# Top-32 attention and an MLP mixer on one core: the ninth tile's last columns copied with its group's, and the first pair's last rows in a buffer of their own

## The chip, the cores and the metric

The kernel runs on one core of one Trainium2 chip. The metric is the device time of one execution in microseconds. Times of the engines come from one profiled execution, whose span runs from the first to the last instruction.

## What is computed

Attention in which each query keeps its 32 largest scores, over 8 batches of 8 heads, 576 positions and head size 64; then a mixer over positions and one over channels:

```python
scores = scale * np.matmul(q, k.transpose(0, 1, 3, 2))           # 8 x 8 x 576 x 576
kth = np.partition(scores, -top_k, axis=-1)[..., -top_k:-top_k + 1]   # top_k = 32
scores = np.where(scores >= kth, scores, -1000000000.0)
attn = np.exp(scores - np.max(scores, axis=-1, keepdims=True))
attn = attn / (np.sum(attn, axis=-1, keepdims=True) + 1e-09)
x = np.matmul(attn, v)           # brought to 8 x 576 x 512, the heads side by side
h = np.maximum(x.transpose(0, 2, 1) @ w_tok1, 0.0) @ w_tok2      # 576 -> 256 -> 576
u = x + h.transpose(0, 2, 1)
out = u + np.maximum(u @ w_ch1, 0.0) @ w_ch2                     # 512 -> 1536 -> 512
```

## The kernel before

**Units and tiles.** The work is cut into 32 units (`plan_unit(u)`): a unit is two heads of one batch, so four units are a batch, and unit 31 is the last pair of batch 7. 576 rows are four tiles of 128 (`W` = 512 columns) and a tail of 64 (`TAIL`). The two heads of a unit give eight tiles of 128 query rows; their two tails of 64 rows together make a ninth tile. The score tiles stand in two groups in SBUF: `SS0` with four tiles (g = 0) and `SS1` with five (g = 1, the ninth tile as its last).

**One unit.** `load_one` brings q and k of both heads by three DMAs each: 512 rows of either head and one for the 64 last rows of both. `qk_tr` turns them on TensorE, `qk_tail_tr` the last rows, and `qk_ev`, `qk_tail_ev` copy them out of PSUM into `qkT`. `s1_mm` makes the last 64 columns of a group's four full tiles (eight products in two banks, one for each head), `s0_mm` the first 512 columns of one tile index, `st_mm` the ninth tile: part 0 its 512 columns, part 1 its last 64, each part in a bank of its own. `s1_ev`, `s0_ev` and `st_ev` copy the banks into `SS0` or `SS1`, on ScalarE (ACT) except in the very first group. Then VectorE (DVE) finds the 32nd largest score of each row: `upper`, `split4`, four `top_round`s and a `low_round` for each group, while GpSimd (POOL) makes the lower halves (`both_bits`, `lower_bits`). ACT makes the exponentials (`expo`) and the terms that suppress what lies below the threshold (`below_act`; `steep` with POOL's `sink`); the result is turned by TensorE (`p_tr`, `ptail_tr`, copied out by `p_ev`, `ptail_ev`) or by a DMA (`turn`), `o_mm` multiplies with v, `o_den` and `o_ev` divide. `h1_mm`, `h1_ev`, `ut_mm`, `ut_ev` are the position mixer for the unit's 128 channels.

**After a batch's fourth unit** `plan_mlp` makes the channel mixer: `h2t_mm`, `h2_mm` and their copies, then `out_mm` with `out_ev` (line 796) for five row blocks of 15 products each. For the last batch the order is another: `plan_part_sums` makes the products over the first three units' channels early (`pre_mm`, line 1103, copied by `pre_ev`), and `plan_mlp_last` adds the fourth (`rest_mm`, `join`), makes `h2_last` and accumulates the output (`begin`, `accum`, line 1156). In the last unit's group 1 the selection is applied by `kept` on DVE (line 574).

**PSUM** has eight banks: two `tp`, three `s0`, one `O`, two `mps`. `st_mm` and, except for the very first group, `s1_mm` and `s0_mm` use `s0`; `mps` serves all of the mixers.

**What sets the order.** All work is entered as tasks into a `Plan` with an engine, an estimated duration, a rank and the things that it waits for. `Plan.order` plays this through, taking on each engine the ready task of the lowest rank, and the instructions are emitted in the order that results; on the chip each engine keeps to it, and semaphores make it wait for data and buffers. A rank is 100 x the unit's number plus an entry of `RANK`. For the last batch, the entry `rush` is added for what follows the selection (`V = U + RANK["rush"]`); for batch 6's mixer `rush6` is added. `slack` is time that the plan adds between a task and what waits for it: the entries `q_wait`, `t_wait`, `o_wait` (in tenths of a us) and a constant for the first units. Where the plan sees TensorE idle before a task, it puts in products that nobody reads (`spare`, line 277), in number:

```python
n = int((now - at) * SPARE / SPARE_US)      # SPARE = 0.8, SPARE_US = 0.22
```

While the plan's time is below 80 us (`SETTLED`) these are four products of 128 columns for each n, later one of 512. `at` is 3.0 us at the start (`LEAD`).

`copy` (lines 336 and 338) is the helper that makes the copies on ACT and on DVE, so many steps share these lines. `lists["hx"]` is a buffer in SBUF that `split4` and `top_round` work in.

Of the kernel before, what the change touches and what calls it, by code (L numbers as in the profile page):

```python
# [19 lines left out]
RANK = {  # L20
    "begin_l": -2054, "o_wait": 16, "t_wait": 6, "q_wait": 272, "v_wait": 112, "pre_mm": -34365, "pre_ev": -31279, "rest_mm": 14920,
    "begin": 31546, "flags": 8794, "rush": -6145, "rush6": -3394, "load": -9078, "qk_tr": 7627, "qk_ev": -3163, "st_mm": -8007,
    "st_ev": 896, "keep": 3463, "h1_mm": -30213, "h1_ev": 3666, "ut_mm": -46945, "ut_ev": -3088, "out_mm": 13329, "out_ev": -772,
# [125 lines left out]
def kernel(  # L149
# [138 lines left out]
    def load_one(st, name, src, b, p, queue=None):  # L288
        queue = queue or nc.sync
        t = ldp.tile([P, NS, 2, D], f32, name=name + "L", tag=name + "L")  # L290
        two = slice(2 * p, 2 * p + 2)
        if isinstance(b, int):
            rws = src[b, two, :, :]
        else:
            rws = src[bass.ds(b, 1), two, :, :].rearrange("o h s d -> (o h) s d")
        for hh in range(2):
            queue.dma_start(
                out=t[:, 0:NT, hh, :], in_=rws[hh, 0:W, :].rearrange("(t p) c -> p t c", p=P)
            )
        queue.dma_start(  # L300
            out=t[0:TAIL, NT, :, :], in_=rws[:, W:S, :].rearrange("h p c -> p h c")
        )
        st[name] = t
# [41 lines left out]
    def qk_tail_tr(st, kind="tp"):  # L345
        tails = bank(kind)[:, 0 : 2 * TAIL].rearrange("p (i c) -> p i c", i=2)
        for i, name in enumerate("qk"):
            nc.tensor.transpose(
                tails[:, i, :],
                st[name][0:TAIL, NT, :, :].rearrange("p h d -> p (h d)"),  # L350
# [7 lines left out]
    def s1_mm(st, g, kind="s0"):  # L358
        T = st["T"]
        x = [bank(kind) for hh in range(2)]  # L360
        for a in range(4):
# [7 lines left out]
            )  # L369
        st["s1"] = x  # L370
# [6 lines left out]
    def s1_ev(st, g, hh, eng="ACT"):  # L377
        copy(
            eng,
            s_tile(st, g)[:, hh:4:2, W:S],  # L380
            st["s1"][hh][:, 0 : 2 * TAIL].rearrange("p (a c) -> p a c", a=2),
        )
# [18 lines left out]
    def st_mm(st, part):  # L401
        T = st["T"]
        lo, hi = ((0, W), (W, S))[part]
        x = bank("s0")
        for hh in range(2):
            nc.tensor.matmul(
                out=x[hh * TAIL : (hh + 1) * TAIL, 0 : hi - lo],
                lhsT=T[rows[hh], 0, W:S],
                rhs=T[rows[hh], 1, lo:hi],
                start=True,  # L410
                stop=True,
            )
        st["st", part] = x

    def st_ev(st, part):
        lo, hi = ((0, W), (W, S))[part]
        nc.scalar.copy(out=st["SS", 1][:, 4, lo:hi], in_=st.pop(("st", part))[:, 0 : hi - lo])
# [438 lines left out]
    def plan_unit(u):  # L856
# [6 lines left out]
        for name, src in (("q", q), ("k", k)):  # L863
            aside = u < 2 and name == "k"
            ld[name] = add("ACT" if aside else "SP", 1.75, U - 5000 if aside else U + RANK["load"],
                           lambda name=name, src=src, aside=aside: load_one(st, name, src, b, p, nc.scalar if aside else None),
                           acq=[("ld" + name, u)])
        ev, prev = [], None
        for i in range(2):
            a = add("PE", 0.61, U + RANK["qk_tr"], lambda i=i: qk_tr(st, i), deps=[ld["qk"[i]], prev] + chain.get("first", []), acq=[("tp", u, "q", i)] + ([] if i else [("qkT", u)]), slack=(3.0 if u == 0 else 4.5) if u < 5 else 0.1 * RANK["q_wait"])  # L870
# [18 lines left out]
        for g in range(2):  # L889
            early = u == 0 and g == 0  # L890
            kind = "mps" if early else "s0"
            a = add("PE", 0.65, U + RANK["s_mm" + str(g)] + 10 * g, lambda g=g, kind=kind: s1_mm(st, g, kind), deps=ev + smm[-1:],
# [3 lines left out]
            for hh in range(2):  # L896
                eng = "DVE" if early and hh else "ACT"
                evs.append(
                    add(eng, 0.17, U + RANK["s_ev" + str(g)] + 10 * g, lambda g=g, hh=hh, eng=eng: s1_ev(st, g, hh, eng),
# [15 lines left out]
            if g == 1:  # L915
                for part in range(2):
                    a = add("PE", (1.01, 0.28)[part], U + RANK["st_mm"], lambda part=part: st_mm(st, part),
                            deps=[smm[-1]], acq=[("s0", u, "st", part)],
                            rel=[("qkT", u)] if part else [])
                    smm.append(a)  # L920
                    evs.append(
                        add("ACT", (0.49, 0.12)[part], U + RANK["st_ev"], lambda part=part: st_ev(st, part),
                            deps=[a, e0] + ([evs[-1]] if part else []),
                            rel=[("s0", u, "st", part)])
                    )
# [361 lines left out]
    with tc.If(flag != 0):  # L1287
        with tc.For_i(0, B, 1) as bv:
            mst = {}
            for p in range(NPAIR):  # L1290
# [9 lines left out]
                for g in range(2):  # L1300
# [7 lines left out]
                    if g == 1:  # L1308
                        for part in range(2):
                            st_mm(st, part)  # L1310
                            st_ev(st, part)
# [62 lines left out]
```

## Time and profile before

| | us |
|---|---|
| median of 3 runs (884.36 to 884.5) | 884.5 |
| the profiled execution | 884.62 |
| its span, first to last instruction | 882.8 |
| busy: VectorE (DVE) | 861.7 |
| busy: ScalarE (ACT) | 834.1 |
| busy: TensorE (PE) | 819.8 |
| busy: GpSimd (POOL) | 597.2 |

The profile names the engines PE (TensorE products), PEld (its weight loads), DVE, ACT, POOL and SP (the queue that issues most DMAs); q behind a name is that engine's sequencer. A group line reads: source line, engine, operation, output tile <- input tiles, shapes, count, then busy time in us, the mean of one in ns, and the idle time before them with what ended it. A line of the timeline or of the chain begins with its start in us from the beginning of the span and its duration. Neighbouring instructions of one engine overlap, so that two back to back take less than twice the time of one. A line of waits reads: who waited, for whom, then the sum in us, the count and the longest. A line of the view by stretches has the stretch, its length, each engine's busy time and instructions, TensorE's granted clock, and the DMA's share and rate.

### The profile page before, as it was taken

The numbers are of one execution on the slowest core, as the hardware profiler recorded it, in microseconds if no ns is written. First come the engines' busy times: TensorE is split into PE (matmuls) and PEld (weight loads), VectorE is DVE, ScalarE is ACT, GpSimd is POOL, SyncE is SP. The second block draws the span as 40 slices with busy tenths as digits, with TensorE's granted clock in tenths as the row PEclk, the third lists the DMA queues.
The fourth block names the chain that finished last, engine by engine and source line by source line (L and its number), as shares of the span: only waits on it lengthen the run. The fifth ranks groups of instructions, "written<-read, shape, count | busy, mean of one in ns | idle before, by whom it ended". The sixth has DMA issues, their size and how long they took to land.

```text
span 882.8 us, 22107 instructions
## 1 busy us (share of the span) xinstructions
PE 819.8 (93%) x7328; PEld 468.6 (53%) x7417; DVE 861.7 (98%) x3850; ACT 834.1 (94%) x1857; POOL 597.2 (68%) x513
## 2 busy tenths in 40 slices
PE   8998988999989999999999999899989999899997
PEld 5666545455545555455554555455555455545552
DVE  8999999999999999999999999999999999999993
ACT  4999999999999999999999999999999999999953
POOL 5679776776877766686676777577667767656700
PEclk9999999999999999999999999999999999999999
DMA  9656764254233453226432552224431453111101
GB/s 129 76 93 83 97 96 77 30 86 83 57 59 42 86 84 83 30 42 121 64 58 38 66 110 57 58 38 90 79 77 31 54 110 55 23 32 43 56 19 58
DMA packets 207483, 58.93 MB, mean 67 GB/s; under 512 B 199809, under 2 KB 202305, under 8 KB 207361
## 3 DMA queue, kind: packets, MB, share of 16 engines
q1 hardware_dynamic: 164320, 48.33, 27.2%
q0 software_dynamic: 40560, 8.46, 11.8%
q8 instruction: 60, 0.98, 0.5%
q10 hardware_dynamic: 2480, 0.66, 0.4%
q14 instruction: 63, 0.51, 0.2%
HBM read 35.78 MB, written 9.44 MB: 51 GB/s over the span
## 4 chain that ended last, share of the span: by engine, by line
ACT 52%; DVE 28%; PE 13%; issue 4%; POOL 2%; DMA 1%; SPq 0%; DVEq 0%; ACTq 0%
ACT SS L336 10%; DVE A L473 7%; ACT E L532 7%; DVE hx L478 6%; ACT U L567 6%; ACT U L550 6%; ACT pb L532 5%; PE mps L788 4%; DVE A L492 4%; ACT pt L605 4%; ACT H2T L754 4%; DVE hi L428 3%; ACT xb L672 3%; ACT qkT L336 2%; DVE hx L460 2%
## 5 line engine op out<-in xcount | busy, mean ns | idle before, releaser
L435 POOL TENSOR_TENSOR lo<-SS 128x1152 int32<-128x1152 int32 x64 | 168.8, 2638 | 241.8 <-DVE A L473 178.0
L473 DVE MAX8 A<-hx 128x8 f32<-128x72 f32 (+2 forms) x1152 | 270.1, 294 | 0.0
L478 DVE MATCH_REPLACE8 hx<-A,hx 128x72 f32<-128x72 f32 (+1 forms) x864 | 199.4, 242 | 0.0
L336 ACT COPY SS<-s 128x512 f32<-128x512 f32 x379 | 171.7, 527 | 5.5 <-PE s L389 5.2
L443 POOL TENSOR_TENSOR lo<-lo,hi 128x1152 int32<-128x1152 int32 x64 | 168.7, 2636 | 0.0
L389 PE MATMUL s<-qkT 64*128 64x512 f32 x508 | 161.6, 640 | 0.4 <-ACT SS L336 0.4
L558 POOL TENSOR_TENSOR SS<-SS,U 128x576 f32<-128x576 f32 x126 | 158.6, 1275 | 0.0
L532 ACT ACTIVATE E<-SS,nmax 128x576 bf16<-128x576 f32 x162 | 129.0, 824 | 1.8 <-POOL nmax L518 1.7
L582 PE MATMUL tp<-identB,E 128*128 128x128 bf16 (+1 forms) x785 | 117.4, 221 | 11.0 <-ACT pt L609 7.6
L567 ACT ACTIVATE U<-SS,A 128x576 bf16<-128x576 f32 x157 | 126.7, 837 | 0.0
L585 PE MATMUL tp<-identN,U 128*128 128x128 bf16 (+1 forms) x785 | 112.7, 220 | 9.9 <-ACT U L567 9.0
L492 DVE MAX8 A<-lo 128x8 f32<-128x296 f32 x288 | 116.9, 452 | 0.0
L550 ACT ACTIVATE U<-SS,kbig 128x576 bf16<-128x576 f32 x126 | 100.0, 822 | 4.0 <-DVE kbig L544 4.0
L788 PE MATMUL mps<-wc2b,H2T 128*128 128x512 bf16 (+1 forms) x402 | 101.9, 380 | 1.9 <-issue 1.4
L532 ACT ACTIVATE pb<-SS,nmax 128x576 bf16<-128x576 f32 x126 | 99.5, 814 | 4.2 <-POOL SS L558 4.0
L585 PEld LDWEIGHTS <-U 128*128 128x128 bf16 (+1 forms) x785 | 77.3, 100 | 37.0 <-ACT U L567 20.5
L428 DVE TENSOR_TENSOR hi<-SS 128x1152 f32<-128x1152 f32 x64 | 96.7, 1511 | 0.1
L582 PEld LDWEIGHTS <-E 128*128 128x128 bf16 (+1 forms) x785 | 75.9, 100 | 30.8 <-issue 20.4
L747 PE MATMUL mps<-UT,wc1b 128*128 128x512 bf16 x311 | 80.1, 380 | 6.1 <-ACT H2T L769 2.1
L605 ACT ACTIVATE pt<-tp 128x512 bf16<-128x512 f32 x130 | 79.0, 635 | 2.2 <-PE tp L580 2.2
L389 PEld LDWEIGHTS s<-qkT 64*128 64x128 f32 x508 | 50.5, 185 | 37.3 <-issue 16.4
L650 PEld LDWEIGHTS <-pt 128*128 128x128 bf16 (+1 forms) x1600 | 60.1, 100 | 19.0 <-issue 10.1
(142 smaller groups left out, 1501.2 us busy)
## 6 DMA issues: line engine op xcount, KB each, us to landing
qL<-in_q_dram SPq DMA_DIRECT2D x64, 128.0 KB, 2.7
kL<-in_k_dram SPq DMA_DIRECT2D x60, 128.0 KB, 2.6
out_dram<-ob SPq DMA_DIRECT2D x28, 256.0 KB, 2.1
vb<-in_v_dram POOLq DMA_DIRECT2D x32, 128.0 KB, 4.4
pt<-pb SPq DMA_TRANSPOSE x126, 2.9
wc1b<-in_moe_w_ch_dram POOLq DMA_DIRECT2D x4, 384.0 KB, 5.7
wc2b<-in_moe_w_ch_dram POOLq DMA_DIRECT2D x4, 384.0 KB, 6.0
qL<-in_q_dram SPq DMA_DIRECT2D x32, 32.0 KB, 2.5
```

The lines of the kernel that those rows point to most:

```text
L336: nc.scalar.copy(out=out, in_=in_)
L389: nc.tensor.matmul(out=x[:, :], lhsT=T[rows[hh], 0, t * P : (t + 1) * P], rhs=T[rows[hh], 1, 0:W], start=True, stop=True,)
L435: nc.gpsimd.tensor_tensor(out=x[:, 0:4, 0:HALF].bitcast(i32), in0=SS[:, 0:4, 0:HALF].bitcast(i32), in1=SS[:, 0:4, HALF:S].bitcast(i32), op ...
L443: nc.gpsimd.tensor_tensor(out=x, in0=x, in1=st["hi"][:, 0:4, :].bitcast(i32), op=ALU.subtract)
L473: nc.vector.max(A[:, i, at], hx[:, i, 0:w])
L478: nc.vector.match_replace(hx[:, i, 0:w], A[:, i, TOP[r] : TOP[r] + 8], hx[:, i, 0:w], NEG)
L532: nc.scalar.activation(out=x, in_=srow(st, i), func=AF.Exp, bias=st["nmax", g][:, a : a + 1], scale=scale,)
L550: nc.scalar.activation(out=U[:, :], in_=srow(st, i), func=AF.Relu, bias=st["kbig", g][:, a : a + 1], scale=-STEEP,)
L558: nc.gpsimd.tensor_tensor(out=x, in0=x, in1=st["U", i][:, :], op=ALU.subtract)
L567: nc.scalar.activation(out=U[:, :], in_=srow(st, i), func=AF.Relu, bias=kcol(st, i), scale=-1.0)
L582: nc.tensor.matmul(out=out, lhsT=st["E", i][:, cols], rhs=identB[:, :], start=True, stop=False)
L585: nc.tensor.matmul(out=out, lhsT=st["U", i][:, cols], rhs=identN[:, :], start=False, stop=True)
```

## The change

- `st_mm` and `st_ev` lose their second part. The ninth tile's last 64 columns are now made in `s1_mm` of group 1, into columns 128 to 191 of that group's first bank, and the copy of this bank (`s1_ev`, first head) takes three pieces of 64 columns instead of two, the third into the ninth tile.
- `load_one` can write the last rows to another place. For unit 0 they go into `lists["hx"]`, and `qk_tail_tr` reads them there.
- In the plan, `slack` of the first unit's `qk_tr` is 2.2 instead of 3.0, the durations of the steps above follow the change, and nearly all entries of `RANK` have other values.

The loop at the end that runs for inputs with ties beyond the lists follows the change of `st_mm`; it is left out below.

```diff
--- before.py
+++ after.py
@@ -18,14 +18,14 @@
 JOINT = 4
 PRE_OF = 12
 RANK = {
-    "begin_l": -2054, "o_wait": 16, "t_wait": 6, "q_wait": 272, "v_wait": 112, "pre_mm": -34365, "pre_ev": -31279, "rest_mm": 14920,
-    "begin": 31546, "flags": 8794, "rush": -6145, "rush6": -3394, "load": -9078, "qk_tr": 7627, "qk_ev": -3163, "st_mm": -8007,
-    "st_ev": 896, "keep": 3463, "h1_mm": -30213, "h1_ev": 3666, "ut_mm": -46945, "ut_ev": -3088, "out_mm": 13329, "out_ev": -772,
-    "h2_mm": 491, "h2_ev": -1235, "h2t_mm": -3315, "h2t_ev": -2228, "pret_mm": 24747, "pret_ev": -21295, "accum": 83593, "s_mm0": -2388,
-    "s_mm1": -2656, "s_ev0": -11066, "s_ev1": -38, "exp_u0": 4024, "exp_u1": 10548, "steep0": 323, "steep1": -6527, "sink0": -6549,
-    "sink1": -5954, "exp_t0": -3794, "exp_t1": -6073, "below0": 2165, "below1": 11963, "p_tr0": 1171, "p_tr1": -26336, "p_ev0": 5579,
-    "p_ev1": -62498, "pt_tr0": -9392, "pt_tr1": -1933, "pt_ev0": 7940, "pt_ev1": 9043, "o_mm0": 8167, "o_mm1": -17681, "o_ev0": -3137,
-    "o_ev1": -655,
+    "begin_l": -2054, "o_wait": 22, "t_wait": 3, "q_wait": 220, "v_wait": 112, "pre_mm": -33481, "pre_ev": -43328, "rest_mm": 20020,
+    "begin": 32009, "flags": 7446, "rush": -4944, "rush6": 6821, "load": -9311, "qk_tr": 8528, "qk_ev": -3205, "st_mm": -7714,
+    "st_ev": 1683, "keep": 4504, "h1_mm": -31045, "h1_ev": 3117, "ut_mm": -43777, "ut_ev": -3181, "out_mm": 13077, "out_ev": -369,
+    "h2_mm": 958, "h2_ev": -1679, "h2t_mm": -3871, "h2t_ev": -1079, "pret_mm": 16364, "pret_ev": -16874, "accum": 83040, "s_mm0": -2734,
+    "s_mm1": -3532, "s_ev0": -11267, "s_ev1": -268, "exp_u0": 3404, "exp_u1": 11223, "steep0": -324, "steep1": -6339, "sink0": -6462,
+    "sink1": -5317, "exp_t0": -3851, "exp_t1": -5454, "below0": 2625, "below1": 11600, "p_tr0": 1530, "p_tr1": -27944, "p_ev0": 6066,
+    "p_ev1": -71079, "pt_tr0": -8725, "pt_tr1": -2104, "pt_ev0": 8280, "pt_ev1": 4230, "o_mm0": 7249, "o_mm1": -17567, "o_ev0": -2897,
+    "o_ev1": -30,
 }
 SPARE_US = 0.22
 LEAD = 3.0
@@ -285,7 +285,7 @@
 
 
 
-    def load_one(st, name, src, b, p, queue=None):
+    def load_one(st, name, src, b, p, queue=None, tail=None):
         queue = queue or nc.sync
         t = ldp.tile([P, NS, 2, D], f32, name=name + "L", tag=name + "L")
         two = slice(2 * p, 2 * p + 2)
@@ -297,10 +297,10 @@
             queue.dma_start(
                 out=t[:, 0:NT, hh, :], in_=rws[hh, 0:W, :].rearrange("(t p) c -> p t c", p=P)
             )
-        queue.dma_start(
-            out=t[0:TAIL, NT, :, :], in_=rws[:, W:S, :].rearrange("h p c -> p h c")
-        )
-        st[name] = t
+        if tail is None:
+            tail = t[0:TAIL, NT, :, :]
+        queue.dma_start(out=tail, in_=rws[:, W:S, :].rearrange("h p c -> p h c"))
+        st[name], st[name, "tail"] = t, tail
 
     def v_piece(mst, b, t):
         if t == 0:
@@ -347,7 +347,7 @@
         for i, name in enumerate("qk"):
             nc.tensor.transpose(
                 tails[:, i, :],
-                st[name][0:TAIL, NT, :, :].rearrange("p h d -> p (h d)"),
+                st[name, "tail"].rearrange("p h d -> p (h d)"),
                 identF[0:TAIL, 0:TAIL],
             )
         st["tails"] = tails
@@ -367,6 +367,12 @@
                 start=True,
                 stop=True,
             )
+        if g:
+            for hh in range(2):
+                nc.tensor.matmul(
+                    out=x[0][hh * TAIL : (hh + 1) * TAIL, 2 * TAIL : 3 * TAIL],
+                    lhsT=T[rows[hh], 0, W:S], rhs=T[rows[hh], 1, W:S], start=True, stop=True,
+                )
         st["s1"] = x
 
     def s_tile(st, g):
@@ -375,10 +381,11 @@
         return st["SS", g]
 
     def s1_ev(st, g, hh, eng="ACT"):
+        n = 3 if g and not hh else 2
         copy(
             eng,
-            s_tile(st, g)[:, hh:4:2, W:S],
-            st["s1"][hh][:, 0 : 2 * TAIL].rearrange("p (a c) -> p a c", a=2),
+            s_tile(st, g)[:, hh : 4 + g : 2, W:S],
+            st["s1"][hh][:, 0 : n * TAIL].rearrange("p (a c) -> p a c", a=n),
         )
 
     def s0_mm(st, t, kind="s0"):
@@ -398,23 +405,17 @@
     def s0_ev(st, t, hh, eng="ACT"):
         copy(eng, s_tile(st, t // 2)[:, 2 * (t % 2) + hh, 0:W], st["s0", t][hh][:, :])
 
-    def st_mm(st, part):
+    def st_mm(st):
         T = st["T"]
-        lo, hi = ((0, W), (W, S))[part]
-        x = bank("s0")
+        x = st["st"] = bank("s0")
         for hh in range(2):
             nc.tensor.matmul(
-                out=x[hh * TAIL : (hh + 1) * TAIL, 0 : hi - lo],
-                lhsT=T[rows[hh], 0, W:S],
-                rhs=T[rows[hh], 1, lo:hi],
-                start=True,
-                stop=True,
-            )
-        st["st", part] = x
-
-    def st_ev(st, part):
-        lo, hi = ((0, W), (W, S))[part]
-        nc.scalar.copy(out=st["SS", 1][:, 4, lo:hi], in_=st.pop(("st", part))[:, 0 : hi - lo])
+                out=x[hh * TAIL : (hh + 1) * TAIL, 0:W], lhsT=T[rows[hh], 0, W:S], rhs=T[rows[hh], 1, 0:W],
+                start=True, stop=True,
+            )
+
+    def st_ev(st):
+        nc.scalar.copy(out=st["SS", 1][:, 4, 0:W], in_=st.pop("st")[:, 0:W])
 
     def gtiles(g):
         return range(4 * g, 4 * g + 4 + g)
@@ -862,12 +863,13 @@
         ld = {}
         for name, src in (("q", q), ("k", k)):
             aside = u < 2 and name == "k"
+            tail = lists["hx"][0:TAIL, "qk".index(name), 0 : 2 * D].rearrange("p (h d) -> p h d", h=2) if u == 0 else None
             ld[name] = add("ACT" if aside else "SP", 1.75, U - 5000 if aside else U + RANK["load"],
-                           lambda name=name, src=src, aside=aside: load_one(st, name, src, b, p, nc.scalar if aside else None),
+                           lambda name=name, src=src, aside=aside, tail=tail: load_one(st, name, src, b, p, nc.scalar if aside else None, tail),
                            acq=[("ld" + name, u)])
         ev, prev = [], None
         for i in range(2):
-            a = add("PE", 0.61, U + RANK["qk_tr"], lambda i=i: qk_tr(st, i), deps=[ld["qk"[i]], prev] + chain.get("first", []), acq=[("tp", u, "q", i)] + ([] if i else [("qkT", u)]), slack=(3.0 if u == 0 else 4.5) if u < 5 else 0.1 * RANK["q_wait"])
+            a = add("PE", 0.61, U + RANK["qk_tr"], lambda i=i: qk_tr(st, i), deps=[ld["qk"[i]], prev] + chain.get("first", []), acq=[("tp", u, "q", i)] + ([] if i else [("qkT", u)]), slack=(2.2 if u == 0 else 4.5) if u < 5 else 0.1 * RANK["q_wait"])
             prev = a
             eng = "DVE" if u == 0 else "ACT"
             ev.append(
@@ -889,14 +891,14 @@
         for g in range(2):
             early = u == 0 and g == 0
             kind = "mps" if early else "s0"
-            a = add("PE", 0.65, U + RANK["s_mm" + str(g)] + 10 * g, lambda g=g, kind=kind: s1_mm(st, g, kind), deps=ev + smm[-1:],
+            a = add("PE", (0.65, 0.86)[g], U + RANK["s_mm" + str(g)] + 10 * g, lambda g=g, kind=kind: s1_mm(st, g, kind), deps=ev + smm[-1:],
                     acq=[(kind, u, g, "s1", 0), (kind, u, g, "s1", 1)])
             smm.append(a)
             evs = []
             for hh in range(2):
                 eng = "DVE" if early and hh else "ACT"
                 evs.append(
-                    add(eng, 0.17, U + RANK["s_ev" + str(g)] + 10 * g, lambda g=g, hh=hh, eng=eng: s1_ev(st, g, hh, eng),
+                    add(eng, 0.22 if g and not hh else 0.17, U + RANK["s_ev" + str(g)] + 10 * g, lambda g=g, hh=hh, eng=eng: s1_ev(st, g, hh, eng),
                         deps=[a] + ([] if early else evs),
                         acq=[] if hh else [(f"SS{g}", u)], rel=[(kind, u, g, "s1", hh)])
                 )
@@ -913,16 +915,11 @@
                             lambda t=t, hh=hh, eng=eng: s0_ev(st, t, hh, eng), deps=[a, e0], rel=[(kind, u, t, hh)])
                     )
             if g == 1:
-                for part in range(2):
-                    a = add("PE", (1.01, 0.28)[part], U + RANK["st_mm"], lambda part=part: st_mm(st, part),
-                            deps=[smm[-1]], acq=[("s0", u, "st", part)],
-                            rel=[("qkT", u)] if part else [])
-                    smm.append(a)
-                    evs.append(
-                        add("ACT", (0.49, 0.12)[part], U + RANK["st_ev"], lambda part=part: st_ev(st, part),
-                            deps=[a, e0] + ([evs[-1]] if part else []),
-                            rel=[("s0", u, "st", part)])
-                    )
+                a = add("PE", 1.01, U + RANK["st_mm"], lambda: st_mm(st), deps=[smm[-1]], acq=[("s0", u, "st")], rel=[("qkT", u)])
+                smm.append(a)
+                evs.append(
+                    add("ACT", 0.49, U + RANK["st_ev"], lambda: st_ev(st), deps=[a, e0], rel=[("s0", u, "st")])
+                )
             n = 4 + g
             x = add("DVE", 0.305 * n + 0.035, U + 5 * g, lambda g=g: upper(st, g), deps=evs + [chain.get("bits")], port=True)
             for y in issue.get((u, g), []):
...
```

More of the change, by code (lines that the diff above doesn't have):

```diff
@@ L1308 @@
                     if g == 1:
-                        for part in range(2):
-                            st_mm(st, part)
-                            st_ev(st, part)
+                        st_mm(st)
+                        st_ev(st)
                     full_select(st, g)
```

## The prediction

> **What bounds the kernel now.** I read the page first: busy shares, then the chain that ended last.
>
> ```profile
> PE 819.8 (93%) x7328; PEld 468.6 (53%) x7417; DVE 861.7 (98%) x3850; ACT 834.1 (94%) x1857; POOL 597.2 (68%) x513
> ACT 52%; DVE 28%; PE 13%; issue 4%; POOL 2%; DMA 1%; SPq 0%; DVEq 0%; ACTq 0%
> ```
>
> The chain gives ACT the larger share, the busy line gives DVE: two engines compete for the bound. The busy time by stretches decides between them, with VectorE's own waits beside it.
>
> ```profile
> core 0: us, PE busy (x) PEld busy (x) DVE busy (x) ACT busy (x) POOL busy (x), PEclk, DMA share, GB/s
> 10.50:120.00 109.50, 101.84 (x1023) 65.43 (x1030) 109.33 (x501) 97.55 (x214) 80.47 (x69) 1.00 0.68 93
> 360.00:480.00 120.00, 113.16 (x967) 61.98 (x981) 119.86 (x544) 120.00 (x269) 82.14 (x69) 1.00 0.41 64
> 720.00:840.00 120.00, 111.91 (x1008) 63.47 (x1021) 119.90 (x547) 118.42 (x267) 80.33 (x69) 1.00 0.23 47
> 840.00:857.00 17.00, 15.80 (x166) 9.35 (x168) 16.41 (x31) 7.74 (x19) 1.44 (x2) 1.00 0.06 12
> 857.00:883.00 26.00, 19.14 (x97) 8.05 (x97) 10.32 (x18) 9.54 (x17) 0.00 (x0) 0.96 0.14 49
> ...
> DVE hx L1199 <- PE s L1156: 6.0, 1, 6.0
> DVE qkT L338 <- PE tp L327: 1.0, 1, 1.0
> ```
>
> From 10.5 to 840 us DVE lacks at most 0.17 us in any stretch. The waits at the top of its list belong to the end (L1199) and to the head (L338), and asked for 10.5 to 840 alone the list is empty. ACT has room in the first stretch (97.55 of 109.50) and a little in the last (118.42 of 120); between them it is just as full as DVE, but it never makes DVE wait. So three parts set the time: a head up to DVE's first `upper` at 10.53, about 830 us of selection on DVE, and an end from the last `low_round` at about 840. Only what shortens DVE's own work, the head or the end can be seen in the time.
>
> **The fused copy.** The rows with its price are these: a copy alone, then two of the same shape back to back, then a 512-column copy with the 64-column one behind it.
>
> ```profile
> 7.91 0.27 ACT L336 COPY SS<-mps 128x128 f32<-128x128 f32 x1 [0.50 <-PE mps L363]
> 8.83 0.59 ACT L336 COPY SS<-s 128x512 f32<-128x512 f32 x1 [0.65 <-PE s L389]
> 10.17 0.44 ACT L336 COPY SS<-s 128x128 f32<-128x128 f32 x2
> 11.54 1.07 ACT L336 COPY SS<-s 128x512 f32<-128x512 f32 x2 [0.93 <-PE s L389]
> 14.35 0.70 ACT L417 COPY SS<-s 128x512 f32<-128x512 f32 x2
> ...
> L406 PE MATMUL s<-qkT 64*64 64x64 f32 x128 | 10.0, 234 | 1.8 <-ACT SS L336 1.8
> ```
>
> Removed per unit: one 128x64 copy. Behind another copy it adds 0.70 - 0.59 = 0.11 us. Added: 64 more columns in the 128x128 copy. A second 128x128 copy adds 0.44 - 0.27 = 0.17, a second 128x512 one 1.07 - 0.59 = 0.48, so a column costs 0.31/384 = 0.8 ns and 64 cost 0.05. Net -0.06 us a unit, -1.9 us of ACT over 32 units. The price is of the same engine, memory and type; the one thing not shown is a source of three 64-column pieces instead of two, and I take no extra for it (bounds: nothing, or at most the 0.17 us of a whole second copy, which would make it +0.12 a unit and +3.8 us of ACT in all).
>
> TensorE issues the same 64x64 products, 10.0/32 = 0.31 us a unit, only earlier: they now stand in front of the copy of group 1's last 64 columns and of its `s0` products. That delays the first evictions of the group by up to 0.3 us. Group 1's scores are needed by an `upper` that stands behind all of DVE's rounds of group 0, and those rounds cover the delay; if they did not, it would cost these 0.3 us a unit. POOL's pass over the same scores comes later still. One bank of three is taken once less per unit. Neither DVE instruction nor DVE byte is removed. Worth in the time: 0, because the saving lies on an engine that never makes DVE wait between 10.5 and 840. The loss would show only where ACT is at 120.00 of 120 and has to fall behind by more than it has in hand; the idle at its end (118.42 of 120) says that it catches up.
>
> **The first pair's last rows.** The first line is of the chain, the others of the timeline.
>
> ```profile
> 1.27 3.61 DMA qL<-in_q_dram
> ...
> 1.00 3.66 PE L277 MATMUL mps<-zeros 128*128 128x128 bf16 x40 [1.00 <-DVE zeros L224]
> 5.01 0.63 PE L327 MATMUL tp<-identF,qL 128*128 128x128 f32 x4 [0.35 <-DMA qL<-in_q_dram]
> 5.68 1.29 DVE L338 COPY qkT<-tp 128x512 f32<-128x512 f32 x2 [1.04 <-PE tp L327]
> 6.89 0.28 DVE L338 COPY qkT<-s 128x128 f32<-128x128 f32 x1
> 7.22 0.66 PE L363 MATMUL mps<-qkT 64*128 64x64 f32 x8 [0.72 <-DVE qkT L338]
> 7.72 1.08 PE L389 MATMUL s<-qkT 64*128 64x512 f32 x4
> 8.63 1.02 PE L389 MATMUL tp<-qkT 64*128 64x512 f32 x4
> 10.53 1.36 DVE L428 TENSOR_TENSOR hi<-SS 128x1152 f32<-128x1152 f32 x1
> ```
>
> The transposes of q start 0.13 us after a load issued at 1.27 has landed (1.27 + 3.61 = 4.88). That load is the second head's 512 rows; the last rows are issued behind it, so the transposes do not wait for them now, and a buffer of their own frees nothing here. The last rows are there before DVE is: its copies L338 run from 5.68 without a break to 7.17 (6.89 + 0.28), the last rows' as the third. The DMA has the same pieces and the same queue. So the new buffer is worth 0 at this place. It also lets the third pair's load into that q buffer start a little earlier, which is off the path: `qk_tr` of that pair comes long after. `hx` is first written by `split4`, behind the `upper` at 10.53, long after the transposes read it.
>
> What does change is the plan's time for `qk_tr`: the load's 1.75, SP's lag of 1.2 and the slack of 3.0 make 5.95, which becomes 5.15. The plan fills PE before it with (5.95 - 3.0) x 0.8/0.22 = 10 lots of four, the 40 of the row; (5.15 - 3.0) gives 7 lots, 28. The data still lands at 4.88, so 12 products fewer save nothing; PE waits longer.
>
> **The order.** The new ranks reorder ACT and PE throughout. DVE covers that until 840; at the end it does not:
>
> ```profile
> 832.89 2.32 PE L788 MATMUL mps<-wc2b,H2T 128*64 128x512 bf16 x10
> 836.52 0.58 ACT L796 COPY ob<-mps 64x512 f32<-64x512 f32 x1
> 836.98 0.40 ACT L704 ACTIVATE H1T<-mps 128x256 bf16<-128x256 f32 x1
> 837.43 0.39 PE L713 MATMUL mps<-w2b,H1T 128*128 128x512 bf16 x1 [0.91 <-ACT H1T L704]
> 838.19 1.46 PE L277 MATMUL O<-w1b,identB 128*128 128x512 bf16 x6
> 838.59 0.79 ACT L532 ACTIVATE pb<-SS,nmax 128x576 bf16<-128x576 f32 x1
> 839.26 0.70 ACT L737 CAST UT<-mps 128x512 bf16<-128x512 f32 x2
> 839.90 2.29 PE L1103 MATMUL mps<-UT,wc1b 128*128 128x512 bf16 x9 [0.25 <-ACT UT L737]
> 846.71 1.46 PE L1103 MATMUL mps<-UT,wc1b 128*128 128x512 bf16 x6 [0.20 <-DVE SS L338]
> 848.10 0.47 PE L580 MATMUL tp<-identB,E 128*64 128x128 bf16 x5
> 850.77 0.82 PE L1103 MATMUL mps<-UT,wc1b 128*128 128x512 bf16 x2
> ```
>
> At 836.52 batch 6's last output copy (L796) goes ahead of unit 30's `h1_ev` (L704), and PE waits 0.91 us for it. The lower rank goes first. Before, L796 has 2800 - 3394 - 772 + 120 = -1246 against 3000 - 6145 + 100 + 3666 = 621 of L704; after, 2800 + 6821 - 369 + 120 = 9372 against 3000 - 4944 + 100 + 3117 = 1273. The order turns, H1T comes 836.98 - 836.52 = 0.46 us earlier, and with it UT and the first `pre_mm`. I count 0.46 (bounds: 0, if DVE's order absorbs it, to 0.46 plus one of the exponentials before UT, 839.26 - 838.59 = 0.67). Nothing else on this path turns: `pre_mm` stays ahead of `p_tr1` in rank.
>
> Sum on the profiled execution: 884.62 (span 882.8 and 1.8 around it) - 0 - 0 - 0.46 = 884.16; the median of the runs lies 0.12 lower, so 884.0 us. About 0.2%, 1.8 us, is what a measurement of this kernel can tell from no change: the forecast lies within that.
>
> **The rivals.** A: the end gains more. The `pre_mm` blocks at 846.71 and 850.77 stand between the last selection and the PV products; the transposes of the last columns (L580) wait for the first until 848.10. With batch 6's MLP ranked 10,000 later, units 28 to 30 may finish earlier and these blocks run before. That takes up to 1.46 + 0.82 = 2.28 us more: 881.8, and 881.1 with an exponential's wait as well. For it: PE fills with nothing (L277, 1.46 us) just before the first `pre_mm`. Against it: the blocks are released by DVE copies, and DVE has no free time there (16.41 of 17.00).
>
> B: slower at the head, by the clock. The fillers (L277) by stretches, those under way at a stretch's beginning counted in; the last columns are the granted clock and the DMA:
>
> ```profile
> 0.95:1.95 1.00, 0.95 (x10) 0.96 (x11) 1.00 0.02 6
> 2.95:3.65 0.70, 0.70 (x10) 0.70 (x8) 1.00 1.27 286
> 3.75:4.45 0.70, 0.70 (x16) 0.70 (x14) 1.00 1.33 231
> ```
>
> Ten products in the first 1.00 us, so 0.1 us each; then 10 and 16 in stretches of 0.70. The pace steps up at about 3.7, 2.7 us after the first filler, though the granted clock reads 1.00 throughout. 28 fillers at 0.1 us last 2.8 us, barely as long. If the pace has not doubled by then, L327, L363 and L389 of the head run at half pace: about 0.5 + 0.5 + 1.9 = 2.9 us more, 886.9. It decides when the step comes after the 28th filler. [...]
>
> C: slower at the end, by batch 6's MLP, now ranked behind. Between its last product (832.89 + 2.32 = 835.21) and the first `pre_mm` at 839.90 lie 4.7 us, and about half of them are fillers (1.46) and waiting (0.91). An output row block is 15 products, at the pace of that L788 row (2.32 us for 10) 3.4 us. So 2.4 us of it can move there for nothing. It decides from there on: a whole row block beyond that holds one of the two `mps` banks of `pre_mm` and costs up to 3.4 us, 887.4. Against it: ACT and PE both run out of work before 840, so what is delayed is made up.
>
> **How the numbers follow.** Forecast 0.45, A 0.33, B 0.10, C 0.12. A counts as faster, B and C as slower, the forecast (no visible effect included) as same. A's chance is high because the order of the end is the only thing that is free to move and it has 2.3 us to give; its lower end, 881.1, is the range's. B's and C's prices are upper bounds, so 886.9 leaves out about half of C and little below.
>
> **What would show it.** The fused copy: L417 without its 128x64 form, ACT about 2 us less busy in all, DVE's busy time unchanged within 1 us and still no wait from its first `upper` to its last `low_round`. The head: 28 fillers, the first `upper` at 10.5 (B: above 11.5, with the transposes of q no earlier). The order: H1T of unit 30 ahead of batch 6's last output copy, the time from the last `low_round` to the end 0 to 1 us shorter (A: over 2 us; C: an L788 behind the first `pre_mm`). The prediction is wrong at its root if DVE shows waits for scores or products between 10.5 and 840: then the order, not DVE's work, sets the time.

## The result and the profile after

The changed kernel takes 888.2 us, the median of 14 executions (885.8 to 888.85), against 885.08 for the kernel before beside it (14, 884.24 to 885.76). The ratio is 1.003, with a 95% interval of 1.0022 to 1.0038: slower, by 3.1 us. The forecast was 884.0, and the range ended at 886.9. The 14 executions stand in two groups: four lie between 885.8 and 886.03, ten between 887.46 and 888.85. The profiled one, 888.56 (span 886.6), belongs to the larger group.

The page's busy line and the shares of the chain, after:

```profile
PE 829.3 (94%) x7419; PEld 469.8 (53%) x7419; DVE 861.9 (97%) x3850; ACT 833.6 (94%) x1825; POOL 597.1 (67%) x513
ACT 54%; DVE 33%; issue 5%; PE 4%; POOL 3%; DMA 1%; SPq 0%; DVEq 0%; ACTq 0%
```

DVE is as busy as before (861.7 then), ACT has lost its 32 copies, yet only 0.5 us. The view by stretches, with the rows that answer to those of before:

```profile
core 0: us, PE busy (x) PEld busy (x) DVE busy (x) ACT busy (x) POOL busy (x), PEclk, DMA share, GB/s
...
360.00:480.00 120.00, 112.79 (x983) 61.72 (x979) 119.90 (x546) 119.95 (x262) 84.06 (x73) 1.00 0.35 62
...
720.00:840.00 120.00, 113.36 (x1044) 64.22 (x1040) 119.83 (x552) 117.62 (x259) 81.69 (x67) 1.00 0.25 49
```

DVE lacks no more than 0.17 us in these stretches, as before. The middle has not changed: from the first `upper` to the first `kept` it is 829.59 us against 829.41. So the loss is at the two ends. The head, from the timeline:

```profile
0.99 3.17 PE L277 MATMUL mps<-zeros 128*128 128x128 bf16 x28 [0.99 <-DVE zeros L224]
...
5.20 1.09 PE L327 MATMUL tp<-identF,qL 128*128 128x128 f32 x4 [1.04 <-DMA qL<-in_q_dram]
...
6.33 0.69 DVE L338 COPY qkT<-tp 128x512 f32<-128x512 f32 x1 [1.69 <-PE tp L327]
...
8.12 1.11 PE L363 MATMUL mps<-qkT 64*128 64x64 f32 x8 [0.58 <-DVE qkT L338]
...
9.03 2.02 PE L396 MATMUL s<-qkT 64*128 64x512 f32 x4
...
10.84 1.81 PE L396 MATMUL tp<-qkT 64*128 64x512 f32 x4
...
13.53 1.36 DVE L429 TENSOR_TENSOR hi<-SS 128x1152 f32<-128x1152 f32 x1
```

TensorE does here what it did before, apart from the number of fillers, 28 instead of 40, and from the place where it reads the last rows. But the four transposes take 1.09 us instead of 0.63, the eight L363 products 1.11 instead of 0.66, the score products 2.02 and 1.81 instead of 1.08 and 1.02. The first `upper` starts at 13.53 instead of 10.53: 3.00 us, of which 0.19 are there before the transposes begin (5.20 against 5.01), because q's load landed later, at 5.07 instead of 4.88. The fillers alone, by stretches:

```profile
0.95:1.95 1.00, 0.96 (x10) 0.96 (x11) 1.00 0.02 5
2.95:3.65 0.70, 0.70 (x10) 0.70 (x8) 1.00 1.28 286
3.75:4.45 0.70, 0.41 (x4) 0.14 (x2) 1.00 1.33 238
```

The pace of before rose at 3.7, from 10 fillers in 0.70 us to 16; here the fillers run out at 4.16 at the first pace, and the products stay at it until 12.42, where the trace has the clock's first recorded step up. The view by stretches shows the granted clock as 1.00 ahead of this step too, in both kernels.

The end, from the timeline, between the first `kept` (L574 and L575) and the outputs' last products (L1156 and L1153). In the kernel before:

```profile
839.94 2.27 DVE L574 SCALAR_TENSOR_TENSOR E<-SS,A,E 128x576 bf16<-128x576 f32 x3
...
865.77 0.43 PE L763 MATMUL mps<-UT,wc1b 128*128 128x64 bf16 x9
...
874.28 2.01 PE L1156 MATMUL tp<-wc2b,H2T 128*128 128x512 bf16 x8
```

In the changed kernel, with two steps ahead of the first `kept`:

```profile
839.04 0.58 ACT L797 COPY ob<-mps 64x512 f32<-64x512 f32 x1
...
840.19 0.38 ACT L705 ACTIVATE H1T<-mps 128x256 bf16<-128x256 f32 x1
...
843.12 2.27 DVE L575 SCALAR_TENSOR_TENSOR E<-SS,A,E 128x576 bf16<-128x576 f32 x3
...
859.39 0.55 PE L764 MATMUL mps<-UT,wc1b 128*128 128x64 bf16 x9
...
860.10 0.59 PE L1164 MATMUL mps<-UT,wc1b 128*128 128x512 bf16 x2
...
877.85 2.01 PE L1153 MATMUL tp<-wc2b,H2T 128*128 128x512 bf16 x8
```

From the first `kept` to the end of the last accumulating product (`accum`) it is 36.73 us against 36.34, and from there to the end of the span 6.79 against 6.47. The sum of the differences is 3.00 + 0.18 + 0.39 + 0.32 = 3.89, against 886.65 - 882.75 = 3.90 between the spans.

### The profile page after: what moved, and what is told of

It is laid out like the page before. It is cut to its first block, busy times and chain, and to the rows that moved or that the text cites. A ratio compares the mean times of both kernels' runs of the same rounds, so it can differ in the third digit from the quotient of the medians.

```text
span 886.6 us, 22181 instructions
## 1 busy us (share of the span) xinstructions
PE 829.3 (94%) x7419; PEld 469.8 (53%) x7419; DVE 861.9 (97%) x3850; ACT 833.6 (94%) x1825; POOL 597.1 (67%) x513
## 4 chain that ended last, share of the span: by engine, by line
ACT 54%; DVE 33%; issue 5%; PE 4%; POOL 3%; DMA 1%; SPq 0%; DVEq 0%; ACTq 0%
ACT SS L336 10%; DVE A L474 8%; DVE hx L479 7%; ACT E L533 6%; ACT U L568 6%; ACT U L551 6%; ACT pb L533 5%; DVE A L493 4%; ACT H2T L755 4%; ACT pt L606 4%; DVE hi L429 4%; ACT xb L673 3%; DVE hx L461 2%; ACT qkT L336 2%; DVE lo L457 2%
## 5 line engine op out<-in xcount | busy, mean ns | idle before, releaser
L396 PE MATMUL s<-qkT 64*128 64x512 f32 x508 | 159.8, 643 | 0.5 <-ACT SS L336 0.5
L583 PE MATMUL tp<-identB,E 128*128 128x128 bf16 (+1 forms) x785 | 113.2, 220 | 19.2 <-ACT pt L610 8.6
L568 ACT ACTIVATE U<-SS,A 128x576 bf16<-128x576 f32 x157 | 123.3, 834 | 0.0
L586 PE MATMUL tp<-identN,U 128*128 128x128 bf16 (+1 forms) x785 | 110.3, 219 | 5.1 <-ACT U L568 4.6
L533 ACT ACTIVATE pb<-SS,nmax 128x576 bf16<-128x576 f32 x126 | 103.0, 818 | 4.0 <-POOL SS L559 3.6
L789 PE MATMUL mps<-wc2b,H2T 128*128 128x512 bf16 (+1 forms) x420 | 104.7, 380 | 0.0
L551 ACT ACTIVATE U<-SS,kbig 128x576 bf16<-128x576 f32 x126 | 97.0, 816 | 4.5 <-DVE kbig L545 4.5
L748 PE MATMUL mps<-UT,wc1b 128*128 128x512 bf16 x336 | 82.7, 380 | 3.1 <-ACT H2T L755 2.6
L606 ACT ACTIVATE pt<-tp 128x512 bf16<-128x512 f32 x130 | 76.9, 651 | 2.2 <-PE tp L581 2.2
L651 PE MATMUL O<-vb,pt 128*128 128x65 bf16 x1575 | 66.1, 195 | 2.5 <-ACT xb L673 2.1
```

The lines of the kernel that those rows point to most:

```text
L396: nc.tensor.matmul(out=x[:, :], lhsT=T[rows[hh], 0, t * P : (t + 1) * P], rhs=T[rows[hh], 1, 0:W], start=True, stop=True,)
L533: nc.scalar.activation(out=x, in_=srow(st, i), func=AF.Exp, bias=st["nmax", g][:, a : a + 1], scale=scale,)
L568: nc.scalar.activation(out=U[:, :], in_=srow(st, i), func=AF.Relu, bias=kcol(st, i), scale=-1.0)
L583: nc.tensor.matmul(out=out, lhsT=st["E", i][:, cols], rhs=identB[:, :], start=True, stop=False)
L586: nc.tensor.matmul(out=out, lhsT=st["U", i][:, cols], rhs=identN[:, :], start=False, stop=True)
```

## Experiments

Each kernel ran in five rounds beside the kernel before. In short, the theories that the expectations weigh. For the head: TensorE stays at the slow pace (1.09 us for the four transposes instead of 0.63) until it has been busy for long enough, and 28 fillers are too few in most executions. What counts may be busy time, a fixed length of work, or the number of products. Against it: the fused copy or the new buffer delays the head by itself. For the end: the new ranks, or again the fused copy.

**Forty fillers in the changed kernel**, `after40` and, on another chip, `after40_again`:

```diff
 def spare(...):
+        if at < 6.0:
+            n = 10
```

> The changed kernel with 40 filler products ahead of the first transposes instead of 28; every other instruction and the order stay. Theory 1 (the filler count sets the clock of the head): the first upper starts at 10.5 to 11.0 us instead of 13.53 and the time falls by 2.5 to 3.0 us from 888.2, to about 885.5; what is left over the kernel before, 0.4 to 0.8 us, stems from the order at the end. Rival (the buffer of the last rows or the plan's earlier head is what costs): the first upper stays at 13 or later and the time at 887.5 to 888.5.

> The changed kernel with 40 fillers once more, on the same chip as the next one, so that the two can be compared: about 885.8, and 36.7 us from the first kept to the last accumulating product.

Measured: 885.82 us against 885.06 before, ratio 1.0007 (0.9998 to 1.0016); again 885.94 against 884.99, 1.0011 (1.0002 to 1.002). None of the 22 executions is over 886.76. The timeline of the second:

```profile
0.99 3.86 PE L279 MATMUL mps<-zeros 128*128 128x128 bf16 x40 [0.99 <-DVE zeros L224]
...
10.51 1.36 DVE L431 TENSOR_TENSOR hi<-SS 128x1152 f32<-128x1152 f32 x1
...
839.92 2.26 DVE L577 SCALAR_TENSOR_TENSOR E<-SS,A,E 128x576 bf16<-128x576 f32 x3
...
856.20 0.55 PE L766 MATMUL mps<-UT,wc1b 128*128 128x64 bf16 x9
...
874.65 2.01 PE L1155 MATMUL tp<-wc2b,H2T 128*128 128x512 bf16 x8
```

The 12 dummy products are worth 2.3 to 2.4 us (888.2 - 885.94 and - 885.82), and the first `upper` is back at 10.51. This is also where the changed kernel's own faster group lies. In the profile of `after40` itself, an execution of 885.88, the clock stepped up at 6.15 instead of 4.08, and the first `upper` is later:

```profile
11.18 1.36 DVE L431 TENSOR_TENSOR hi<-SS 128x1152 f32<-128x1152 f32 x1
```

What is left over the kernel before, 0.8 to 0.95 us in the medians, shows between profiles of like heads too: 885.23 here against 884.62 before (first `upper` at 10.51 and 10.53), and 885.88 against 885.01 of `before_fused` below (11.18 and 11.07). So it is not of the head.

**Twenty-eight fillers in the kernel before**, `before28` (`n = 7` in the same place):

> The kernel before with 28 filler products instead of 40, nothing else. Theory 1: in most executions the first upper comes about 3 us later than 10.53 and the time is 887 to 888.2. Rival (ranks and buffer cost, not the fillers): 885, as before.

Measured: 887.61 against 885.06, ratio 1.0026 (1.0016 to 1.0037). Of eight executions six lie at 887.53 to 888.05, one at 886.06 and one at 884.64; the last is the profiled one:

```profile
0.99 3.17 PE L279 MATMUL mps<-zeros 128*128 128x128 bf16 x28 [0.99 <-DVE zeros L224]
...
4.95 0.63 PE L329 MATMUL tp<-identF,qL 128*128 128x128 f32 x4 [0.79 <-DMA qL<-in_q_dram]
...
10.46 1.36 DVE L430 TENSOR_TENSOR hi<-SS 128x1152 f32<-128x1152 f32 x1
```

So the loss comes without the fused copy and without the buffer, and it is a matter of the execution: here the same 28 fillers at the same slow pace are followed by transposes at the full one (0.63), and nothing is lost. The clock's recorded step up is at 4.69 here, behind the last filler's end at 4.16. A length of work that is the same in every execution would not part the executions of one program in this way.

**Number or busy time**, `before_half40`: 40 fillers of half the size.

```diff
-        for _ in range(n * 512 // w):
+        n, m = n * 512 // w, P
+        if at < 6.0:
+            wide, w, m = zeros[:, 0:TAIL], TAIL, TAIL
+        for _ in range(n):
-                out=banks[r][i][:, 0:w], lhsT=(...)[:, :], rhs=wide, ...
+                out=banks[r][i][0:m, 0:w], lhsT=(...)[:, 0:m], rhs=wide, ...
```

> The kernel before with its 40 first fillers on 64 columns and 64 weight columns instead of 128: the same number, about half the busy time. Theory 1a (TensorE's busy time before the transposes decides): late executions as with 28 fillers or more, the median at 887.5 or above. Rival 1c (the number of products decides): 885, as before.

Measured: 887.43 against 884.99, ratio 1.0026 (1.0016 to 1.0036), all nine executions between 887.01 and 887.86.

```profile
0.99 2.35 PE L280 MATMUL mps<-zeros 128*64 128x64 bf16 x40 [0.99 <-DVE zeros L224]
...
4.87 1.09 PE L330 MATMUL tp<-identF,qL 128*128 128x128 f32 x4 [1.54 <-DMA qL<-in_q_dram]
...
13.31 1.36 DVE L431 TENSOR_TENSOR hi<-SS 128x1152 f32<-128x1152 f32 x1
```

Forty products that end at 3.34 never raise the pace in time: it is not their number.

**How many are enough**, `before32` and `before36` (`n = 8` and `n = 9`):

> The kernel before with 32 fillers instead of 40. With 28, 7 of 8 executions were about 2.7 us late, with 40 none of 52. [...] Rival 1b (a fixed length of unbroken work is needed, the same in each execution): all at 885 or all at 887.5.

> The kernel before with 36 fillers instead of 40: at 0.107 us each they end at about 4.85, just before the transposes at 4.95 to 5.01. Theory 1a: few or none of the executions late, the median at 885.0, and the slowest below those of 40 fillers, since fillers no longer hold up the transposes in executions in which the pace steps up late. Rival 1b: all at 885, or all at 887.5.

Measured against 885.13: 884.85 for 32, ratio 1.0000 (0.9991 to 1.0009), with two of eleven executions at 886.13 and 886.2; 885.09 for 36, 0.9999 (0.999 to 1.0008), none over 885.4. The profiled execution of `before32` is one of the two, and it shows something else:

```profile
1.00 3.25 PE L279 MATMUL mps<-zeros 128*128 128x128 bf16 x32 [1.00 <-DVE zeros L224]
...
4.93 0.63 PE L329 MATMUL tp<-identF,qL 128*128 128x128 f32 x4 [0.68 <-DMA qL<-in_q_dram]
...
7.13 1.12 PE L365 MATMUL mps<-qkT 64*128 64x64 f32 x8 [0.78 <-DVE qkT L340]
...
8.04 2.02 PE L391 MATMUL s<-qkT 64*128 64x512 f32 x4
```

The transposes at 4.93 run at full pace (0.63), the products from 7.13 on at half (1.12, 2.02). Its stretches:

```profile
core 0: us, PE busy (x) PEld busy (x) DVE busy (x) ACT busy (x) POOL busy (x), PEclk, DMA share, GB/s
4.00:6.00 2.00, 1.32 (x13) 0.91 (x10) 0.94 (x3) 0.02 (x1) 2.00 (x3) 1.00 1.34 213
6.00:8.00 2.00, 1.22 (x11) 1.06 (x12) 1.08 (x3) 1.27 (x1) 0.38 (x1) 0.79 1.89 183
8.00:10.00 2.00, 2.00 (x10) 0.97 (x10) 0.29 (x1) 0.27 (x1) 0.00 (x0) 0.50 2.57 154
10.00:12.00 2.00, 2.00 (x19) 1.22 (x16) 1.38 (x2) 1.31 (x4) 0.00 (x0) 0.86 1.43 201
```

The trace's records of the clock have the pace stepping up at 3.74, down at 7.15 and up again at 10.57, 3.41 and 3.42 us from one to the next. In three other profiles the clock is full, from the first step up to the fall behind the last products, for 870.40 us (the changed kernel), 873.81 (`after40`) and 877.23 (the kernel before), which are 3.41 and 3.42 us apart again. What sets this distance is not shown. The step is not tied to the program's start, since with 40 fillers the first one lies anywhere between 3.67 and 6.21.

What decides the pace is less clear. TensorE was busy for 1.95 of the 3.41 us up to 7.15, and the pace fell; with 2.34 of the 3.42 us from 3.99 to 7.41 (`before_hx`) it held. In the kernel before, the step up at 3.67 came after 2.67 us of fillers, but in the changed kernel 2.84 us of transposes and 64-row products between 5.59 and 9.01 brought none. So how busy TensorE is counts (the 2.35 us of half-size fillers in `before_half40` brought no step in time either), but its busy time as the profile has it is not the whole measure.

**The two edits one at a time**, in the kernel before: `before_fused` (the fused copy, in the old order: the second part's tasks stay in the plan and do nothing) and `before_hx` (only the new buffer).

```diff
 s1_mm:
+        if g:
+            for hh in range(2):
+                nc.tensor.matmul(
+                    out=x[0][hh * TAIL : (hh + 1) * TAIL, 2 * TAIL : 3 * TAIL], ...)
 s1_ev:
+        n = 3 if g and not hh else 2
         ...
 st_mm:
-        for hh in range(2):
+        for hh in range(2) if part == 0 else ():
 st_ev:
+        if part == 0:
+            nc.scalar.copy(...)
```

```diff
+            tail = lists["hx"][0:TAIL, ...] if u == 0 else None      # load_one: the last rows' target
```

> The kernel before with the fused copy alone: the two 64-column products of the ninth tile in group 1's first bank, one copy of 192 columns, the plan's tasks for the old second part kept as empty ones, so that the order of all the rest is that of before. Theory 1: ACT about 2 us less busy in all, and no change of the time, within 0.3 us of before, since DVE sets it between 10.5 and 840. Rival (the two products delay the first evictions of group 1): DVE shows waits for scores, and the time rises by up to 0.3 us a unit, 9 us in all.

> The kernel before with the first pair's last rows in hx, nothing else: 40 fillers, the old ranks, the old second part. Theory 1: no change, within 0.3 us of before; the transposes of q start at about 5.0. Rival (the buffer acts on the loads of the head): the first upper moves by 0.3 us or more.

Measured against 885.06: 884.94 with the fused copy, ratio 0.9997 (0.9988 to 1.0006); 885.21 with the buffer, 0.9999 (0.999 to 1.0008). Neither changes the time. The busy line of `before_fused`, then from its groups by shape the fused copy and an ordinary copy of 128 columns:

```profile
PE 824.7 (93%) x7328; PEld 474.7 (54%) x7417; DVE 861.3 (98%) x3850; ACT 833.0 (94%) x1825; POOL 596.4 (68%) x513
```

```profile
L336 ACT COPY SS<-s 128x192 f32<-128x192 f32 x32 | 11.3, 354 | 0.7 <-PE s L372 0.5 <-DVE SS L338 0.2
```

```profile
L336 ACT COPY SS<-s 128x128 f32<-128x128 f32 x94 | 23.8, 295 | 0.1
```

ACT gains 834.1 - 833.0 = 1.1 us with the order held. The fused copy takes 354 ns and one of 128 columns 295, so 64 more columns add 59 ns; in the changed kernel it is 355 and 305, 50 ns. That is close to the 0.05 us that the prediction had worked out.

**What the order costs.** `after40_pret` and `after40_pret_again` are `after40` with the old rank of one step, nine products of 64 columns in the last batch (`"pret_mm": 24747` for 16364), which the new ranks put ahead of the first `rest_mm`:

> The changed kernel with 40 fillers and the entry pret_mm of RANK at its old value; in the instruction order only the 64-column products of the last two sums move, from before the last unit's remaining products to behind them, with three copies and additions that depend on them. In the runs so far the time from the first kept to the last accumulating product is 36.73 us in the changed kernel, with 28 or 40 fillers, and 36.29 to 36.34 in all others. Theory 2 (nine such products stand between UT and the first rest_mm, 0.39 us): 36.3 us here, and the time 0.4 us below that of the changed kernel with 40 fillers, about 885.4. Rival (batch 6's mixer or the seventh batch's ranks make the end longer): 36.7 us and 885.8.

> The same with pret_mm at its old value, once more. Theory 2: 36.3 us in that part again, and a median 0.4 us below its neighbour's. Rival (the part that follows, from the last product to the end of the program, gives the 0.4 us back): the same median within 0.2 us, and a longer last part in the profile.

Measured: 886.0 against 885.13, ratio 1.0011 (1.0001 to 1.002); again 885.91 against 884.99, 1.0011 (1.0002 to 1.002), on the same chip as `after40_again` with its 885.94. From the timeline of the second:

```profile
840.18 2.26 DVE L577 SCALAR_TENSOR_TENSOR E<-SS,A,E 128x576 bf16<-128x576 f32 x3
...
866.00 0.42 PE L766 MATMUL mps<-UT,wc1b 128*128 128x64 bf16 x9
...
874.51 2.01 PE L1155 MATMUL tp<-wc2b,H2T 128*128 128x512 bf16 x8
```

The nine products move from 856.20 to 866.00, and the way from the first `kept` to the end of the last accumulating product falls from 36.74 to 36.33, which is what the kernel before needs (36.34). So the trace names 0.4 us of the end. The total does not fall, and both signs of the rival are there: like medians (885.91 and 885.94) and a longer last part. From the last product to the end of the span it is 7.30 us here and 7.50 in the other profile, against 6.66 and 6.57 without the edit, and 6.47 to 6.82 in all twelve profiles without it. The traces behind the views show where the time goes. VectorE's last drain, an instruction that the views do not count as busy, starts 1.08 and 0.83 us after the instruction before it in the two profiles with the edit, and 0.11 us in the twelve others. GpSimd's next closing step comes 0.82 and 0.57 us after GpSimd's own drain, instead of 0.04: more than the 0.4 us that was gained. Why VectorE's drain comes late is not shown.

`after_oldrank` puts all of the old ranks (and the old slack) into the changed kernel, `before_newrank` the new ranks into the kernel before:

> The changed kernel with the old RANK and the old slack of 3.0, so 40 fillers; the fused copy and the buffer stay, and the plan makes a new order of them. In the kernel before, the new ranks alone cost 18 us. Theory 3 (ranks fit one plan alone, since any shorter task makes another order): several us slower than 885, with waits of DVE between 10.5 and 840 or a longer end. Rival (the new ranks are bad by themselves): 885 to 886.

> The kernel before with the changed kernel's RANK; 40 fillers, the old second part and the old place of the last rows. Theory 2: no difference between 10.5 and 840 us, the time from the first kept to the last accumulating product 36.7 us, the time about 885.6, 0.4 to 0.8 over before. Rival (what is left over the kernel before comes from the fused copy in this order, not from the ranks): 885.0 and 36.3 us.

Measured: 887.16 against 884.99 for the first, ratio 1.0026 (1.0015 to 1.0036); 903.4 against 885.13 for the second, 1.0205 (1.0191 to 1.0219), where 885.6 was expected. In the first the way from the first `kept` to the last accumulating product is 37.40 us instead of 36.34, and the middle 829.96. In the second DVE waits, in this list of its waits:

```profile
DVE hx L1199 <- PE s L1156: 7.5, 1, 7.5
DVE rden L662 <- PE O L650: 6.7, 5, 3.3
DVE SS L1178 <- ACT qkT L1113: 3.7, 1, 3.7
DVE SS L338 <- PE mps L1103: 3.4, 4, 2.6
```

Five waits of DVE for `o_mm` products cost 6.7 us, and four of them, 4.5 us, lie in the middle, which grew to 837.20; from the first `kept` to the last accumulating product it is 46.80. The longest of the five, 3.3 us, ends at 505.38. TensorE stands idle there for 5.62 us up to 503.60, and the granted clock is 0.51 from 500.6 to 507.5, so a part of the loss in this profile is slower products. A set of ranks fits one plan. With the ninth tile's last columns as tasks of their own the new ranks cost 18 us; without these tasks the old ones cost 2.2 over the kernel before and 1.2 over `after40_again`, which ran on the same chip. So the new ranks are the better of the two for the changed kernel, and still end 0.8 to 0.95 above the kernel before.

No kernel here beats the one before by more than its interval. The nearest is `before_fused`, at 0.9997.

## Why the prediction was wrong

**The step that failed** is "so 12 products fewer save nothing; PE waits longer". It counted the fillers as work that ends before data arrives, and so as free in both directions. They are what raises TensorE's pace: with 40 of them the first step up was recorded at 3.67 in the kernel before, with 28 at 12.42 in the changed one. With 12 fewer the head is 3.00 us longer in the profiled execution and the time 2.3 to 2.55 us in the median (`after40`, `before28`). The rows for it stood in the prediction, and rival B had the head at half pace and a price of 2.9 that comes close to the 3.00 of the profile. What was mis-sized is its chance: 0.10, because the pace of the one trace had stepped up after 2.7 us, just before 28 fillers end (they were put at 2.8 us and took 3.17). One trace shows one draw. In nine profiles with 40 fillers the step came at 3.67 (the kernel before), 3.99 (`before_hx`) and 4.08 (`after40_again`), and in the six others between 5.27 and 6.21. With 28 it came at 4.69 in one profile and at 12.42 in the other. The loss fell on 10 of 14 executions with 28 fillers, and on six or seven of eight in `before28`.

From the forecast of 884.0 to the 888.2 measured it is 4.2 us. The fillers are 2.3 to 2.4 of them and the order 0.8 to 0.95, where the sum had -0.46. The rest, about 0.6, is the base: the three runs of the kernel before that the sum started from had a median of 884.5, and fourteen have 885.08.

**The order**: the 0.46 us did not come. The ranks were read right, but the order in the trace did not turn: the last output copy of batch 6 (L797) still starts at 839.04 and `h1_ev` (L705) at 840.19. A lower rank decides only between tasks that are ready at the same time in the plan, and I did not establish that both were. Instead another pair turned, one that I did not look at: `pret_mm` (16364 + ...) went ahead of `rest_mm` (20020 + ...), 24747 against 14920 before. It shows as 0.4 us in the trace.

**Right**: the fused copy is worth nothing and so is the buffer; each alone shows it. The chain of reasons holds too: no wait of DVE between its first `upper` and 840, and DVE's busy time within 0.2 us. ACT was to fall by 1.9 us and fell by 0.5 (1.1 with the order held); the term was too large, and as ACT does not set the time, that cost nothing.

**The other rivals**: A, a gain at the end, did not come; the end grew by 0.4 up to the last product. C, batch 6's mixer spilling into the end, is not in the timeline: its last output copy is done before the first `kept`.

**Open**: of the 3.1 us the fillers account for 2.3 to 2.4. The remaining 0.8 to 0.95 is put down to the new order, since neither edit alone costs anything; that is by elimination, and it is small: the interval of `after40` just includes no change (0.9998), that of `after40_again` just leaves it out (1.0002). Of it 0.4 us is seen ahead of the last product and goes when the nine products move back, but in the total it does not show, because VectorE's last drain came later in both profiles with that edit. What the rest consists of is open.

## What to carry to other kernels

Work that computes nothing can still set the time, here 2.3 to 2.4 us for 12 products: before removing or shortening warm-up products, read whether the pace of the products behind them depends on them, and how far the step lies from their end in several executions. A schedule's constant that is tightened "because the data comes earlier" changes everything that is derived from it, here the number of fillers through `n`. Ranks tuned for one set of tasks are part of that set: test an edit with the order held, or the reordering is measured with it.

## What the runs showed of the hardware

TensorE's step to full pace differs between executions of one program: it came at 6.15 us in `after40` and at 4.08 in `after40_again` on another chip. With 40 fillers in front it lay between 3.67 and 6.21 in nine profiles, and the first `upper` followed it, at 10.51 to 10.61 where the step came by 4.08 and at 10.74 to 11.26 where it came from 5.27 on. With 28 fillers (about 3 us of work) it came at 12.42 in one profile and at 4.69 in the other. With 32 it came at 3.74, and the pace fell back at 7.15 for 3.42 us (granted clock 0.50 from 8 to 10 us); with 36 and 40 no profile shows such a fall in the head.

The granted clock in the view by stretches does not show the first, slow part: it reads 1.00 over fillers 0.1 us apart and over a head whose transposes take 1.09 us instead of 0.63. The records of the clock begin with its first step up, at 3.67 in the kernel before and at 12.42 in the changed one. The view does show the fall in `before32` (0.79, 0.50, 0.86).
